# Group normalisation on one core: the store of the last tile but one in four parts on two queues

## The chip, the core and the metric

The kernel runs on one core of a Trainium2 chip. The metric is the device time of one execution in microseconds (us). The kernel before was run three times: 631.46, 631.93 and 632.73 us, so its median is 631.93 us. One further execution was recorded by the hardware profiler; it took 633.28 us, and all durations below come from it.

## The reference

The input `x` has 128 samples of 1024 channels of 32 x 16 values in bfloat16. The channels of a sample form 32 groups of 32 channels. Each group is normalised by its own mean and variance, and each channel is then scaled and shifted:

```python
xr = x.reshape(B, G, C // G, H, W)                   # G = 32
mu = xr.mean(axis=(2, 3, 4), keepdims=True)
var = ((xr - mu) ** 2).mean(axis=(2, 3, 4), keepdims=True)
xn = (xr - mu) / jnp.sqrt(var + 1e-5)
out = xn.reshape(B, C, H, W) * g[None, :, None, None] + b[None, :, None, None]
```

Input and output are 134 MB each, and every byte of them crosses between HBM and SBUF once.

## The kernel before, in words

**Tiles.** A tile is four samples: 4 x 32 groups lie on the 128 partitions, and each partition (a "row" below) holds the 32 x 512 = 16384 values of one group, 32,768 bytes, which lie together in HBM. A tile is 4 MB, and there are 32 (`NT`), numbered 0 to 31. Six buffers `x0` to `x5` (`SLOTS`) hold tiles in turn. A tile is normalised in place and stored from the buffer that it was loaded to.

**Work on one tile.** TensorE adds up the tile by 32 matmuls into one PSUM bank (`sums`). ScalarE makes a rough mean of one channel and then four passes of squares over the tile (`squares`, L228). VectorE joins the two to mean, variance, scale and shift (`normalise`, L244 to L284), and then writes 32 pieces of 128 x 512 in place (L294); the last of these raises `s_done` of the buffer.

**Queues.** All transfers of the kernel before are issued by SyncE (SP), in an order written out by hand (L147 to L155): the load of tile 0, two small loads of `g` and `b`, the loads of tiles 1 to 5; and then for every tile its store, followed by the load of the tile that comes five later. `load` (L132) waits until the store that last used the buffer has landed; `store` (L138) waits for `s_done` and issues one transfer of 128 rows (L141). After the last store, SP raises `s_gone` (L156) and waits until every buffer's stores have landed (L158); that wait ends the kernel. The two small loads read their source through `four`, which puts a dimension of four samples with step 0 in front, so that their outermost count is 4.

**GpSimd** makes the identity matrix at the start (L164 and L174), issues no transfer, waits for `s_gone` (L333) and clears semaphores.

A transfer raises its semaphore by 16 in all, whatever its size.

The functions that the change touches:

Of the kernel before, what the change touches and what calls it, by code (L numbers as in the profile page):

```python
# [11 lines left out]
BF16 = mybir.dt.bfloat16  # L12
# [4 lines left out]
SLOTS = 6  # L17
# [5 lines left out]
def kernel(  # L23
# [20 lines left out]
    NT = B0 // NS  # L44
# [4 lines left out]

    FIRST = -NT % SLOTS  # L50
    ROUNDS = (NT + FIRST) // SLOTS

    x_v = x.rearrange("(t n) (q k) h w -> t (n q) (k h w)", n=NS, q=G)
    o_v = out.rearrange("(t n) (q k) h w -> t (n q) (k h w)", n=NS, q=G)
# [7 lines left out]
    def sb(name, shape, dtype):  # L62
        return ctx.enter_context(nc.sbuf_tensor(name, shape, dtype))
# [7 lines left out]
    xs = [sb(f"x{j}", [P, F], BF16) for j in range(SLOTS)]  # L71
# [14 lines left out]
    ja = sb("ja", [P, HW], BF16)  # L86
    js = sb("js", [P, SQ], BF16)
    jd = sb("jd", [P, MM_FREE], BF16)
    jv = sb("jv", [P, SQ_PARTS], F32)

    def small(name, n=1):
# [13 lines left out]
    def sems(name):  # L105
        return [sem(f"{name}{j}") for j in range(SLOTS)]
# [13 lines left out]
    s_done = sems("done")  # L120
# [5 lines left out]
    s_eye = sem("eye")  # L126
    s_store = [tc.alloc_semaphore(f"store{j}") for j in range(SLOTS)]
    s_gone = tc.alloc_semaphore("gone")

    sp, pe, act, dve, pool = nc.sync, nc.tensor, nc.scalar, nc.vector, nc.gpsimd  # L130

# [6 lines left out]
    def store(i):  # L138
        j, n = (i + FIRST) % SLOTS, i // SLOTS
        sp.wait_ge(s_done[j], n + 1)  # L140
        sp.dma_start(out=o_v[i], in_=xs[j][:]).then_inc(s_store[j], 16)  # L141

    def four(v):
        return bass.AP(tensor=v.tensor, offset=v.offset, ap=[[0, NS]] + list(v.ap))
# [7 lines left out]
    for i in range(NT):  # L152
        store(i)
        if i >= 1 and i + SLOTS - 1 < NT:
            load(i + SLOTS - 1)  # L155
    sp.sem_inc(s_gone, 1)  # L156
    for j in range(SLOTS):
        sp.wait_ge(s_store[j], 16 * len(range((j - FIRST) % SLOTS, NT, SLOTS)))  # L158


    dve.memset(eps_t[:], EPS).then_inc(s_eps, 1)  # L161
# [3 lines left out]
        out=half[:],  # L165
        in_=ones[:],
# [8 lines left out]
        out=eye[:],  # L175
        in_=half[:],
# [128 lines left out]

    with pe.Fori(16, 16 * ROUNDS + 1, 16) as n16:
        m16 = pe.snap(n16 - 16)
# [5 lines left out]

    with act.Fori(1, ROUNDS + 1) as n:
        n16 = act.snap(n * 16)
        m, m16 = act.snap(n - 1), act.snap(n16 - 16)
# [5 lines left out]

    with dve.Fori(1, ROUNDS + 1) as n:
        m = dve.snap(n - 1)
# [5 lines left out]

    pool.wait_ge(s_gone, 1)  # L333
    pool.sem_clear(range(all_sems[0].num, all_sems[-1].num + 1))

# [29 lines left out]
```

## Time and profile before

| what | value |
|---|---|
| median of three runs | 631.93 us |
| the profiled execution, whole | 633.28 us |
| its span, as the profiler shows it | 631.6 us |
| bytes moved | 268.50 MB, 425 GB/s over the span |
| share of the 16 DMA engines' time that is busy | 98.9% |
| busiest compute engine | ACT, 519.4 us (82%) |
| VectorE | 394.9 us (63%) |
| TensorE | 287.4 us (46%) |
| GpSimd | 0.8 us |

How to read it: the span runs from the first to the last recorded instruction, and the whole time has 1.7 us more around it. The profile's chain of waits gives for the end of the execution what each step waited for. The view by stages gives for a stretch of the span the busy time of each engine and, in the last two columns, the share of the 16 DMA engines that was busy (1.00 is all of them; a packet is counted in the stretch in which it starts) and the GB/s that they moved. The trace also lists every DMA packet with its start, duration, size and queue, though not the DMA engine that moved it. Of the big transfers one packet is one row of 32,768 bytes; a transfer ends on each engine with one packet of 4 bytes, which counts up the semaphore.

### The profile page before, as it was taken

The page shows a single profiled execution, that of the slowest core. Times are in us where ns is not written, and L with a number is a line of the kernel's source. Part 1 is how long each engine was busy: PE and PEld are TensorE (multiplying, and loading weights), DVE is VectorE, ACT ScalarE, POOL GpSimd, SP SyncE. Part 2 cuts the span into 40 slices and gives each one's busy share as a digit, 9 for nine tenths or more (in the row PEclk, how much of TensorE's full clock was granted, in tenths as well). Part 3 has the DMA queues.
Part 4 walks back from the last instruction along what each step waited for, and adds up shares of the span by engine and source line. Part 5 has one row for each costly group of instructions (what it writes and reads, how often), then busy time and mean ns, then how long its engine had stood idle before and what let it go on. Part 6 is the DMA issues. An engine that isn't in the chain of part 4 may idle for free.

```text
span 631.6 us, 2995 instructions
## 1 busy us (share of the span) xinstructions
PE 287.4 (46%) x1024; PEld 3.3 (1%) x32; DVE 394.9 (63%) x1316; ACT 519.4 (82%) x354; POOL 0.8 (0%) x6
## 2 busy tenths in 40 slices
PE   1967605553255532455324654346553455533400
PEld 0000000000000000000000000000000000000000
DVE  0177777666666677777555775556765557755560
ACT  2999999999999999997879887889887898888800
POOL 0000000000000000000000000000000000000000
PEclk9999758756787667876678776777766787667755
DMA  8999999999999999999999999999999999999995
GB/s 363 432 430 417 436 436 432 430 430 434 428 432 432 432 432 432 430 432 430 430 434 434 436 432 432 438 434 436 430 431 434 434 432 432 434 432 432 432 432 235
DMA packets 9484, 268.50 MB, mean 425 GB/s; under 512 B 1288, under 2 KB 1288, under 8 KB 1288
## 3 DMA queue, kind: packets, MB, share of 16 engines
q1 hardware_dynamic: 9480, 268.46, 98.9%
q14 instruction: 3, 0.02, 0.0%
q8 instruction: 1, 0.02, 0.0%
HBM read 134.23 MB, written 134.22 MB: 425 GB/s over the span
## 4 chain that ended last, share of the span: by engine, by line
DMA 73%; ACT 18%; DVE 4%; issue 1%; SPq 1%; DVEq 0%; ACTq 0%
DMA out_dram<-x 67%; ACT js L228 17%; DMA x<-in_x_dram 7%; DVE x L294 3%; ACT ja L217 1%; SPq L136 1%; ACT std L237 0%; DVE jv L268 0%; DVE nd L259 0%; DVE d L255 0%; DVE bia L284 0%; DVE scl L280 0%; DVEq L58 0%; DVE rstd L278 0%; DVEq L254 0%
## 5 line engine op out<-in xcount | busy, mean ns | idle before, releaser
L228 ACT ACTIVATE js<-x,nshift 128x4096 bf16<-128x4096 bf16 x128 | 474.7, 3708 | 4.1
L294 DVE TENSOR_SCALAR x<-x,scl,bia 128x512 bf16<-128x512 bf16 x1024 | 333.7, 406 | 1.2
L193 PE MATMUL ps<-x,eye 128*128 128x512 bf16 x992 | 275.3, 447 | 0.0
L209 PE MATMUL ps<-x,eye 128*128 128x512 bf16 x32 | 18.6, 581 | 303.8 <-DMA x<-in_x_dram 303.8
L255 DVE TENSOR_TENSOR d<-negmean,nshift 128x1 f32<-128x1 f32 x32 | 5.1, 159 | 167.7 <-ACT js L228 167.7
L217 ACT ACTIVATE ja<-x 128x512 bf16<-128x512 bf16 x32 | 20.0, 624 | 48.7 <-DMA x<-in_x_dram 48.0
L244 DVE TENSOR_SCALAR_CACHE_REDUCE jd<-ps 128x512 bf16<-128x512 f32 x32 | 22.0, 686 | 16.4 <-PE ps L193 16.3
L237 ACT ACTIVATE std<-var,eps_t 128x1 f32<-128x1 f32 x32 | 9.4, 295 | 25.8 <-DVE jv L268 25.8
L228 ACT ACTIVATION_READ_ACCUMULATOR js<-x,nshift 128x1 f32 x128 | 23.9, 186 | 0.0
L278 DVE RECIPROCAL rstd<-std 128x1 f32<-128x1 f32 x32 | 5.2, 164 | 11.6 <-ACT std L237 11.6
L284 DVE SCALAR_TENSOR_TENSOR bia<-scl,negmean,bet 128x32 f32<-128x32 f32 x32 | 8.1, 252 | 1.1
L280 DVE TENSOR_SCALAR scl<-gam,rstd 128x32 f32<-128x32 f32 x32 | 7.7, 241 | 1.1
L186 DVE CAST gam<-gam_b 128x32 f32<-128x32 bf16 x1 | 0.2, 181 | 12.9 <-DMA bet_b<-in_b_dram 12.9
L268 DVE TENSOR_SCALAR_CACHE_REDUCE jv<-sq,nd 128x4 f32<-128x4 f32 x32 | 7.0, 217 | 1.1
L259 DVE TENSOR_SCALAR nd<-d 128x1 f32<-128x1 f32 x32 | 6.8, 214 | 1.1
L209 PEld LDWEIGHTS ps<-x,eye 128*128 128x128 bf16 x32 | 3.3, 103 | 578.7 <-DMA x<-in_x_dram 578.7
L217 ACT ACTIVATION_READ_ACCUMULATOR ja<-x 128x1 f32 x32 | 6.0, 187 | 0.0
L268 DVE DVE_READ_ACCUMULATOR jv<-sq,nd 128x1 f32 x32 | 2.7, 83 | 0.0
L244 DVE DVE_READ_ACCUMULATOR jd<-ps 128x1 f32 x32 | 2.6, 82 | 0.0
L184 ACT ACT_TABLE_LOAD x1 | 1.3, 1283 | 1.0 <-ACTq L58 1.0
L161 DVE MEMSET eps_t<- 128x1 f32 x1 | 0.1, 59 | 1.1 <-ACTq L58 1.1
L164 POOL TENSOR_SCALAR_AFFINE_SELECT half<-ones 128x128 bf16<-128x128 bf16 x1 | 0.3, 292 | 0.9 <-DVE ones L162 0.9
(8 smaller groups left out, 1.2 us busy)
## 6 DMA issues: line engine op xcount, KB each, us to landing
x<-in_x_dram SPq DMA_DIRECT2D x32, 4096.0 KB, 29.2
out_dram<-x SPq DMA_DIRECT2D x32, 4096.0 KB, 38.3
gam_b<-in_g_dram SPq DMA_DIRECT2D x1, 8.0 KB
bet_b<-in_b_dram SPq DMA_DIRECT2D x1, 8.0 KB
```

The source lines that it names most:

```text
L136: sp.dma_start(out=xs[j][:], in_=x_v[i]).then_inc(s_load[j], 16)
L193: return pe.add_instruction(mybir.InstMatmult(name=nc.get_next_instruction_name(), ins=[pe.lower_ap(rhs), first.ins[1]], outs=[first.outs[0]],
L209: m = pe.matmul(out=ps[j][:], lhsT=eye[:], rhs=xs[j][:, 0:MM_FREE], start=True, stop=False)
L217: act.activation(out=ja[:], in_=xs[j][:, 0:HW], func=ACT.Identity, scale=-1.0 / HW, accum_out=nshift[j][:],).then_inc(s_shift[j], 1)
L228: act.activation(out=js[:], in_=xs[j][:, k * SQ : (k + 1) * SQ], func=ACT.Square, bias=nshift[j][:], scale=1.0, accum_out=sq[j][:, k : k + 1],
L237: act.activation(out=std[j][:], in_=var[j][:], func=ACT.Sqrt, bias=eps_t[:], scale=1.0).then_inc(s_std[j], 1)
L244: dve.tensor_scalar(out=jd[:], in0=ps[j][:], scalar1=-inv_n, scalar2=None, op0=ALU.mult, op1=ALU.add, accum_out=negmean[j][:],).then_inc(s ...
L259: dve.tensor_scalar(out=nd2[j][:], in0=d[j][:], scalar1=d[j][:], scalar2=-1.0, op0=ALU.mult, op1=ALU.mult,).then_inc(s_nd2[j], 1)
L268: dve.tensor_scalar(out=jv[:], in0=sq[j][:], scalar1=inv_n, scalar2=nd2[j][:], op0=ALU.mult, op1=ALU.add, accum_out=var[j][:],).then_inc(s ...
L280: dve.tensor_scalar(out=scl[j][:], in0=gam[:], scalar1=rstd[j][:], scalar2=None, op0=ALU.mult).then_inc(s_scl[j], 1)
L284: dve.scalar_tensor_tensor(out=bia[j][:], in0=scl[j][:], scalar=negmean[j][:], in1=bet[:], op0=ALU.mult, op1=ALU.add,).then_inc(s_bia[j], 1)
L294: v = dve.tensor_scalar(out=xs[j][:, k * HW : (k + 1) * HW], in0=xs[j][:, k * HW : (k + 1) * HW], scalar1=scl[j][:, k : k + 1], scalar2=bi ...
```

## The change

Only the transfers around the store of tile 30 (`SHAPED = NT - 2`) are touched. SP issues rows 0 to 63 and rows 114 to 127 of that tile as two transfers in place of one. GpSimd issues rows 64 to 88 and rows 89 to 113, each as a transfer of 25 rows whose HBM side is written as 5 x 5 rows. Before the first of these GpSimd issues a load of 5 rows of 64 bytes into a new small tile `turn`, and between the two a load of one value of 2 bytes. GpSimd waits for `s_done` of tile 30 before its first 25 rows. SP's waits at the end also ask for the second part of that store and for the four transfers of GpSimd. The values computed are the same, and so is the order of all other transfers.

```diff
+    SHAPED = NT - 2
...
+    turn = sb("turn", [6, 32], BF16)
...
+    s_turn = tc.alloc_semaphore("turn")
+    s_fives = tc.alloc_semaphore("fives")
...
     def store(i):
         j, n = (i + FIRST) % SLOTS, i // SLOTS
         sp.wait_ge(s_done[j], n + 1)
-        sp.dma_start(out=o_v[i], in_=xs[j][:]).then_inc(s_store[j], 16)
+        if i != SHAPED:
+            sp.dma_start(out=o_v[i], in_=xs[j][:]).then_inc(s_store[j], 16)
+            return
+        rows(sp, i, 0, 64)
+        rows(sp, i, 114, 14)
+
+    def rows(engine, i, r, m):
+        j = (i + FIRST) % SLOTS
+        engine.dma_start(out=o_v[i][r : r + m], in_=xs[j][r : r + m]).then_inc(s_store[j], 16)
+
+    def fives(i, r):
+        j = (i + FIRST) % SLOTS
+        pool.dma_start(
+            out=o_v[i][r : r + 25].rearrange("(a b) f -> a b f", a=5), in_=xs[j][r : r + 25]
+        ).then_inc(s_fives, 16)
...
     for j in range(SLOTS):
-        sp.wait_ge(s_store[j], 16 * len(range((j - FIRST) % SLOTS, NT, SLOTS)))
+        uses = len(range((j - FIRST) % SLOTS, NT, SLOTS))
+        parts = 1 if j == (SHAPED + FIRST) % SLOTS else 0
+        sp.wait_ge(s_store[j], 16 * (uses + parts))
+    sp.wait_ge(s_turn, 32)
+    sp.wait_ge(s_fives, 32)
...
+    j = (SHAPED + FIRST) % SLOTS
+    pool.dma_start(out=turn[0:5, :], in_=x_v[0][0:5, 0:32]).then_inc(s_turn, 16)
+    pool.wait_ge(s_done[j], SHAPED // SLOTS + 1)
+    fives(SHAPED, 64)
+    pool.dma_start(out=turn[5:6, 0:1], in_=x_v[0][5:6, 0:1]).then_inc(s_turn, 16)
+    fives(SHAPED, 89)
+
     pool.wait_ge(s_gone, 1)
```

## The prediction

> **What bounds the kernel.** I read the share of the DMA engines first, then SP's waits at the end, then the end of the span by stages. The page's slices and queues:
>
> ```profile
> DMA  8999999999999999999999999999999999999995
> ...
> q1 hardware_dynamic: 9480, 268.46, 98.9%
> ...
> q8 instruction: 1, 0.02, 0.0%
> ...
> DMA 73%; ACT 18%; DVE 4%; issue 1%; SPq 1%; DVEq 0%; ACTq 0%
> ```
>
> The DMA engines are busy in every slice but the last, and 73% of the chain that ended last is DMA. ACT, the busiest compute engine at 82%, has slack. So only fewer or better placed bytes can help, and the one slice with room is the last. SP's waits from 600 us on, and the stages of the end (the last two columns are the DMA share and GB/s):
>
> ```profile
> SPq L158 <- DMA out_dram<-x: 19.5, 3, 9.6
> ...
> 590.90:610.30 19.40, 0.29 (x2) 0.00 (x0) 12.38 (x41) 7.28 (x5) 0.00 (x0) 0.56 1.01 434
> 610.30:623.00 12.70, 0.00 (x0) 0.00 (x0) 0.00 (x0) 0.00 (x0) 0.00 (x0) 0.50 0.98 423
> 623.00:624.20 1.20, 0.00 (x0) 0.00 (x0) 0.00 (x0) 0.00 (x0) 0.00 (x0) 0.50 0.32 137
> 624.20:626.60 2.40, 0.00 (x0) 0.00 (x0) 0.00 (x0) 0.00 (x0) 0.00 (x0) 0.50 0.25 109
> 626.60:629.00 2.40, 0.00 (x0) 0.00 (x0) 0.00 (x0) 0.00 (x0) 0.00 (x0) 0.50 0.13 55
> 629.00:631.60 2.60, 0.00 (x0) 0.00 (x0) 0.00 (x0) 0.00 (x0) 0.00 (x0) 0.50 0.00 0
> ```
>
> SP waits 19.5 us at L158 for stores; nothing else is at work after 610.3. Until 623.0 all 16 DMA engines are busy (0.98). Then 0.32 x 16 = 5 packets start in 1.2 us, then four (0.25), then two (0.13): a few engines end up to 6 us after the rest, and the kernel waits for the last of them.
>
> Which they are I worked out from the trace's list of packets. In it a row of 32,768 bytes takes 1.213 us, and the next packet of the same engine starts 4 ns before that end, so one row costs 1.21 us. Strung end to start, the packets form 16 chains; each has 512 rows, 8 for every transfer of 128 rows, and one 4-byte packet after each 8. The ends of the chains, in us of the span:
>
> ```
> 11 chains    623.16 to 623.74 (the median of all 16 is 623.54)
>  1 chain     624.76   loses 1.4 us at 469.6 us, beside the only packet of queue q8 (16,384 bytes, 0.93 us)
>  4 chains    627.07, 628.85, 628.86, 629.90
> ```
>
> The four late chains lose 0.1 to 0.6 us at a time, all along the execution, in rows that take longer than 1.213 us: 4.8 to 7.0 us in sum, against 1.3 to 2.1 us for the others. The 256 packets of 64 bytes (the loads of `g` and `b`, outermost count 4) lie on four chains, three of them late ones. The fourth late chain and the fourth 64-byte chain can have changed places in the stringing near 60 us, where all rows took 1.3 to 2.4 us and two chains can't be told apart. I take them as one: **the four engines that served the loads with outermost count 4 are the four that end late.** I call them the first four.
>
> **The change part by part.** All 128 rows of tile 30 still go out, so the bytes stay; their share per engine changes.
>
> *Rows per engine.* 128 rows went to 16 chains and a count of 4 to four chains, so I read a transfer as spread over as many engines as its outermost count allows, up to 16, beginning with the first. Then 64 rows give 4 to each of 16, and 14 rows give one to each of the first 14. A transfer of 5 x 5 rows gives five rows to each of five engines. No row shows GpSimd's queue, nor which five it takes; the diff's counts 5, 5, 1, 5 add up to 16, so if the turns go round, the first small load takes engines 0 to 4, the first 25 rows 5 to 9, the single value 10, the second 25 rows 11 to 15. Of tile 30:
>
> ```
> engines        rows before   rows after    change
> 0-4, 10             8        4+1   =  5    -3 rows = -3.63 us
> 5-9, 11-13          8        4+1+5 = 10    +2 rows = +2.42 us
> 14, 15              8        4+5   =  9    +1 row  = +1.21 us
> ```
>
> The sum is 6 x 5 + 8 x 10 + 2 x 9 = 128.
>
> - *The late four* lose three rows: the last ends at 629.90 - 3.63 = 626.27.
> - *Ordinary engines with ten rows* end at 623.74 + 2.42 = 626.16 at the latest.
> - *The engine of the q8 packet* isn't among the first four. Of the other 12, eight get ten rows: if it is one of these, it ends at 624.76 + 2.42 = **627.18**. With nine rows it ends at 625.97, with five earlier than the rest.
>
> I take the likelier, 627.18, as the new end: 629.90 - 627.18 = **2.72 us** less. If that engine isn't one of the eight, the late one sets the end and the gain is 3.63 us.
>
> *Do the rows come in time?* Tile 30 is ready at 590.9 (SP's issue at 590.92), while an ordinary engine ends tile 31 at 623.54 and so begins tile 30 at 623.54 - 16 x 1.21 = 604.2. GpSimd has 13 us to issue four transfers; SP's issues take 0.33 to 0.72 us each in the trace. GpSimd's own price isn't in the trace: its lower bound is nothing, and even 5 us for each 25 rows stays under the cover. Beyond that cover, up to the issue of tile 31 at 610.3, a heavy engine would still find its other rows to do. Cover gone altogether would cost at most the five rows moved there, 6.05 us.
>
> *Light engines 4 and 10* end tile 30 at about 604.2 + 5 x 1.21 = 610.2; tile 31 is issued at 610.27, and the first load's first packet started 1.0 us after its issue. They idle 1 us and still end near 621: nothing.
>
> *SP* issues one transfer more (0.33 us) at 591.3, before it waits until 610.25 for tile 31: hidden. Its two added waits at L158 follow the waits for the last stores; the three such waits in the trace took 17 to 28 ns each, so under 0.1 us. Behind them stands only the end of the program.
>
> *The two small loads.* Packets of 64 bytes took 11 ns; five of them and the 4-byte ones cost an engine under 0.2 us even at ten times that. The first is issued behind L174, which ends at 2.0 us, with nothing behind it on GpSimd until 590.9; the second lies in the cover above. GpSimd's wait for `s_done` holds up only its own transfers and the clearing of semaphores, which waits for `s_gone` at 610.6 anyway.
>
> *Reading 64 rows through 16 engines.* Before, each engine moved the same rows of SBUF every time; now engines 0 to 15 all read from the lower half of the partitions, and ten of them also from the upper. If they get in each other's way, rows grow longer. Bounds: nothing, as a row took 1.21 us in load and store alike; or twice, the longest rows in the trace (2.43 us near 60 us). I take nothing, since 97% of the rows took 1.225 us or less, and keep the other for a rival. The Trainium skill speaks against me here: "SBUF — State Buffer", section "Door 1: The DMA port swizzle", says that partitions 0 to 63 reach only 8 of 16 ports, with 196 GB/s measured for 64 partitions against 328 for 128 (1 MiB each). By that page the 64 rows would run at about half rate, which would add some 4 rows, 4.8 us, and turn the gain into a loss of 2 us; no row of this trace has 16 engines reading half the partitions.
>
> The same skill ("DMA: Bandwidth & Descriptors", "Why a DMA increments its semaphore by 16 and not by 1") states that GpSimd's transfers on fewer than 16 engines take consecutive ones from a cursor that goes round. It also reports that some of GpSimd's plain copies are put on 16 engines with the rows rounded up, which would leave the cursor where it was; no run here shows either yet.
>
> **The sum.** 633.28 - 2.72 = 630.56 for the profiled execution. The median of the plain runs stands 1.35 us lower (631.93); the same gain gives **629.2 us**, 0.43% less. If all of that 1.35 us were lateness that only the profiled execution has, the last engine would end at 628.55 in plain runs and the gain would be 1.37 us: 630.6.
>
> **The rivals.**
>
> 1. *Shared reading, slower.* Rows of the 64-row part take up to twice as long. For: the packets near 60 us show that a row can take 2.43 us when all engines are disturbed. Against: everywhere else 16 engines hold 1.21 us. Price: four rows of 1.21 us more bring the heavy engine with the q8 packet to 627.18 + 4.84 = 632.02, 2.1 us after the old end: 634.0. If all ten rows of a heavy engine doubled, 627.18 + 12.1 = 639.28: 641.3. It decides once the four rows take 0.68 us more each (2.72 / 4).
> 2. *The turns stand otherwise, slower.* If the first 25 rows fall on late engines, the last ends at 629.90 + 2.42 = 632.32: 634.3. For: nothing in the trace fixes where the turns start. Against: the counts add to 16, so they start alike in each execution.
> 3. *The parts aren't spread as read.* If GpSimd's rows are dealt over all engines, the late ones keep eight rows (no change, 631.9) or get nine (+1.21, 633.1).
> 4. *The lateness isn't there to win.* It grows by chance in single rows; in plain runs it can be smaller or lie on another engine: 630.7 to 631.9.
>
> **Chances.** A measurement of this kernel tells about 0.2% (1.3 us) from no change. The forecast as worked out 0.50 (0.02 of it within 0.2%); rival 1 0.24; rival 2 0.12; rival 3 0.09 (0.05 no change, 0.04 slower); rival 4 0.05. So faster 0.48, same 0.02 + 0.05 + 0.05 = 0.12, slower 0.24 + 0.12 + 0.04 = 0.40. The likeliest case has 628.0 to 630.7: from 3.63 us of gain and a little less lateness, to the 1.37 us above. The range takes in rival 2, rival 3 and rival 1 with its four rows: 628.0 to 636.0. It leaves out the dearer half of rival 1 (0.12) and about 0.04 elsewhere.
>
> **What would show it.** Right: in the profile after, the DMA share falls from full to nothing within some 3 us around 624 to 627, not 6; strung packets show five rows of tile 30 on the four late chains; rows after 591 us keep 1.21 us. Rival 1: rows of 1.5 to 2.4 us after 591 us, and fewer GB/s there than 434. Rival 2: chains with ten rows among the late four, and an end near 632. Rival 3: no chain with five rows. Rival 4: the late chains are within 3 us of the others. My forecast is wrong if rows of the shaped tile slow down by over 0.68 us each, or if an engine of the late four gets GpSimd's rows.

## The result and the profile after

The changed kernel takes 648.53 us (median of four runs, 647.1 to 650.95) against 632.33 us before: 1.0261 times as long, interval 1.0221 to 1.0301. It is 16.2 us slower where 2.7 us of gain were forecast, and beyond the range of 628.0 to 636.0.

The page of the changed kernel, its slices of DMA share and GB/s and its queues:

```profile
DMA  8999999999999999999999999999999999999993
GB/s 366 439 421 417 423 437 433 429 441 423 437 431 429 441 423 435 437 421 445 429 429 441 425 437 433 429 443 423 434 439 425 445 423 435 437 423 402 289 253 156
...
q1 hardware_dynamic: 9444, 266.82, 97.3%
q0 software_dynamic: 160, 1.64, 1.1%
```

Up to the last slice the DMA engines are as busy as before, but in the three slices ahead of it they move 402, 289 and 253 GB/s at a share of 9 tenths or more. Busy engines that move less: that is the reading to learn here. GpSimd's queue is q0; its 1.64 MB are the 50 rows. The same by stages (the last two columns are DMA share and GB/s):

```profile
590.90:604.00 13.10, 0.00 (x0) 0.00 (x0) 6.75 (x24) 5.97 (x5) 0.45 (x1) 0.63 1.08 360
604.00:617.00 13.00, 0.00 (x0) 0.00 (x0) 4.93 (x16) 0.00 (x0) 0.00 (x0) 0.50 0.94 270
617.00:629.00 12.00, 0.00 (x0) 0.00 (x0) 0.00 (x0) 0.00 (x0) 0.00 (x0) 0.50 1.01 246
629.00:635.00 6.00, 0.00 (x0) 0.00 (x0) 0.00 (x0) 0.00 (x0) 0.00 (x0) 0.50 0.86 300
635.00:641.00 6.00, 0.00 (x0) 0.00 (x0) 0.00 (x0) 0.00 (x0) 0.00 (x0) 0.50 0.47 202
641.00:646.00 5.00, 0.00 (x0) 0.00 (x0) 0.00 (x0) 0.00 (x0) 0.00 (x0) 0.50 0.14 59
```

And of the kernel before, the stage to compare with:

```profile
604.00:617.00 13.00, 0.00 (x0) 0.00 (x0) 6.24 (x20) 0.00 (x0) 0.00 (x0) 0.50 1.01 434
```

With the share near 1, 434 GB/s became 270 and 246. The list of packets says how: of the 440 rows that start after 591 us, 143 took longer than 1.3 us (before: one of 437), and the longest 5.29 us. Strung end to start, no chain has gaps of more than 1 us in sum; the rows themselves are long. Their excess over 1.213 us sums to 216.8 us, 13.5 us for each of 16 engines. The chains end 13.7 us later on average (638.5 against 624.8 us) and the last at 645.9.

GpSimd itself was in time (its instructions in the changed kernel; L158 is the transfer of 25 rows):

```profile
589.84 0.52 POOL L158 DMA_DIRECT2D out_dram<-x  x1 [587.21 <-DVE x L317]
590.35 0.50 POOL L361 DMA_DIRECT2D turn<-in_x_dram  x1
590.84 0.51 POOL L158 DMA_DIRECT2D out_dram<-x  x1
```

It issued within 1.5 us, and its first row started at 594.25 us, 4.4 us after the issue, still beside tile 29.

### The profile page after: what moved, and what is told of

Same layout as the page of the kernel before. It is cut to its first block, busy times and chain, and to the rows that moved or that the text cites. A ratio compares the mean times of both kernels' runs of the same rounds, so it can differ in the third digit from the quotient of the medians.

```text
span 648.1 us, 3001 instructions
## 1 busy us (share of the span) xinstructions
PE 286.9 (44%) x1024; PEld 3.3 (1%) x32; DVE 394.7 (61%) x1316; ACT 519.3 (80%) x354; POOL 2.9 (0%) x10
## 3 DMA queue, kind: packets, MB, share of 16 engines
q0 software_dynamic: 160, 1.64, 1.1%
## 4 chain that ended last, share of the span: by engine, by line
DMA 71%; ACT 17%; DVE 4%; issue 1%; SPq 1%; DVEq 0%; ACTq 0%
DMA out_dram<-x 65%; ACT js L251 16%; DMA x<-in_x_dram 6%; DVE x L317 3%; ACT ja L240 1%; SPq L140 1%; ACT std L260 0%; DVE jv L291 0%; DVE nd L282 0%; DVE d L278 0%; DVE bia L307 0%; DVE scl L303 0%; DVEq L59 0%; DVE rstd L301 0%; DVEq L277 0%
## 5 line engine op out<-in xcount | busy, mean ns | idle before, releaser
L158 POOL DMA_DIRECT2D out_dram<-x x2 | 1.0, 516 | 587.2 <-DVE x L317 587.2
```

## The experiments

All change only the store of tile 30 (two repeat a small load instead). Times are medians, compared with the kernel before on the same chip; the ratio stands with its 95% interval.

| run | what goes out for tile 30 | us | before | ratio |
|---|---|---|---|---|
| e1 | SP: rows 0-63, then 64-127 | 647.10 | 632.13 | 1.024 (1.0215 to 1.0265) |
| e2 | SP: two halves of the columns | 632.75 | 632.13 | 1.0007 (0.9995 to 1.0019) |
| e3 | SP: even rows, then odd rows | 632.27 | 632.13 | 1.0003 (0.9992 to 1.0014) |
| e4 | GpSimd: the whole tile | 632.38 | 632.13 | 1.0007 (0.9994 to 1.0019) |
| e5 | SP: eight times 16 rows | 648.97 | 631.90 | 1.0262 (1.0241 to 1.0283) |
| e6 | the change's counts, every second row | 638.35 | 631.90 | 1.0099 (1.0079 to 1.0118) |
| e7 | e6, small loads in another order | 638.11 | 631.90 | 1.0091 (1.0069 to 1.0114) |
| e8 | SP rows 0-63 beside GpSimd 64-127 | 646.13 | 631.90 | 1.025 (1.0196 to 1.0304) |
| e9 | SP even rows beside GpSimd odd rows | 632.08 | 632.01 | 0.9998 (0.9987 to 1.0009) |
| e10 | SP: an eighth of the columns as 4 x 32 rows | 632.46 | 632.01 | 1.0003 (0.9993 to 1.0012) |
| e11 | e6, GpSimd's rows in ten fives | 650.82 | 632.01 | 1.029 (1.027 to 1.0309) |
| e12 | 16 more loads of `g`, at one place | 640.65 | 632.67 | 1.0123 (1.0106 to 1.014) |
| e13 | 16 more loads of `g`, one per tile | 636.20 | 631.86 | 1.0066 (1.0053 to 1.008) |

**Which part stretches the rows?** My theory after the result was rival 1, shared reading; the rivals were GpSimd's queue and the mere cutting of a store. e1 takes GpSimd away and keeps the halves:

```diff
-        sp.dma_start(out=o_v[i], in_=xs[j][:]).then_inc(s_store[j], 16)
+        sp.dma_start(out=o_v[i][0:64], in_=xs[j][0:64]).then_inc(s_store[j], 16)
+        sp.dma_start(out=o_v[i][64:128], in_=xs[j][64:128]).then_inc(s_store[j], 16)
```

> Tile 30 is stored by SP alone, rows 0 to 63 and then rows 64 to 127; GpSimd issues nothing. Theory A (shared reading): 16 engines read half of the partitions at a time, each row of tile 30 takes up to twice 1.21 us, so 8 x 1.21 = 9.7 us at most: 632.3 + 9.7 = 642 us, with rows of about 2.4 us before the end. Rival B (GpSimd's queue is what costs): no GpSimd rows, so as before, 632 us and rows of 1.21 us.

Measured: 15.0 us slower, without any GpSimd row. The stages of e1:

```profile
604.00:617.00 13.00, 0.00 (x0) 0.00 (x0) 5.37 (x17) 0.00 (x0) 0.00 (x0) 0.50 1.02 282
617.00:629.00 12.00, 0.00 (x0) 0.00 (x0) 0.00 (x0) 0.00 (x0) 0.00 (x0) 0.50 0.88 254
```

The same picture as the change: share 1.02, 282 GB/s. The chains end 8.8 us later on average, near the 9.7 us of doubled rows, but the last 12.2 us later in the profiled executions: the load is uneven, and single rows took up to 5.07 us. The halves alone nearly account for the result. e2 cuts by columns instead:

```diff
+        sp.dma_start(out=o_v[i][:, 0 : F // 2], in_=xs[j][:, 0 : F // 2]).then_inc(s_store[j], 16)
+        sp.dma_start(out=o_v[i][:, F // 2 : F], in_=xs[j][:, F // 2 : F]).then_inc(s_store[j], 16)
```

> Tile 30 is stored by SP in two transfers of all 128 rows, the first and the second half of the columns: as many bytes per transfer as in the halves by rows, but each engine reads its usual rows. Theory A (shared reading): as before, 632 us, packets of 16,384 bytes at 0.6 us. Rival C (a store cut in two costs in itself, whichever way): slower by as much as the halves by rows.

Measured: as before within the interval. Two transfers of 2 MB cost nothing if each holds all rows; rival C falls. e3 takes 64 rows at a time, but every second one:

```diff
+        sp.dma_start(out=o_v[i][0:P:2], in_=xs[j][0:P:2]).then_inc(s_store[j], 16)
+        sp.dma_start(out=o_v[i][1:P:2], in_=xs[j][1:P:2]).then_inc(s_store[j], 16)
```

> Tile 30 is stored by SP in two transfers of 64 rows, the even rows and then the odd rows, so that each transfer spans all partitions. Theory A1 (an engine pays when it reads where another engine reads at that moment, whatever the span): rows of tile 30 still meet in pairs, up to 9.7 us more, 638 to 642 us. Rival A2 (only the half of the partitions counts: a transfer that spans all of them is as fast as before): 632 us.

Measured: as before; theory A1 was wrong here. The stage of e3 that answers to e1's:

```profile
604.00:617.00 13.00, 0.00 (x0) 0.00 (x0) 4.27 (x14) 0.00 (x0) 0.00 (x0) 0.50 0.98 423
```

The same count, size and queue as e1, 423 GB/s in place of 282, and one row above 1.3 us. So 64 rows are not slow; 64 neighbouring rows are. e4 gives the whole tile to GpSimd:

```diff
+    pool.wait_ge(s_done[j], (NT - 2) // SLOTS + 1)
+    pool.dma_start(out=o_v[NT - 2], in_=xs[j][:]).then_inc(s_pool, 16)
```

> Tile 30 is stored whole, all 128 rows in one transfer, by GpSimd's queue in place of SP's. Theory A (shared reading): every engine reads its usual rows, so as before, 632 us, rows of 1.21 us; GpSimd's later start (its rows came 4.4 us after its issue) lies under the rest of tile 29. Rival B (GpSimd's queue costs): slower by 6 us or more.

Measured: as before. GpSimd's queue costs nothing in itself here.

**How fine is the grain?** e5 issues eight times 16 neighbouring rows:

```diff
+        for r in range(0, 128, 16):
+            sp.dma_start(out=o_v[i][r : r + 16], in_=xs[j][r : r + 16]).then_inc(s_store[j], 16)
```

> Tile 30 is stored by SP in eight transfers of 16 rows, 0 to 15, 16 to 31 and so on, one row for each engine. Theory H (each half of the partitions, 0 to 63 and 64 to 127, can be read at the rate of eight engines): the rate is as for the halves by rows, 216 GB/s while 16 engines read one half, and successive transfers of one half behave alike: about 642 to 648 us. Rival P (each small group of partitions can be read at the rate of one engine only, and 16 rows lie on four such groups): rows of four times 1.21 us, 3 x 9.7 = 29 us more, 655 to 662 us.

Measured: 649.0 us, 17.1 us slower: a little above theory H, well below rival P. Rows took up to 8.58 us, more than in e1, so something finer than the two halves probably counts as well. That the price stays below rival P may be because the engines drift apart and do not all read the same rows at once; no run shows that alone. Neither price was right. e8 puts the halves on two queues at the same time:

```diff
+            sp.dma_start(out=o_v[i][0:64], in_=xs[j][0:64]).then_inc(s_store[j], 16)
...
+    pool.dma_start(out=o_v[NT - 2][64:128], in_=xs[j][64:128]).then_inc(s_pool, 16)
```

> Rows 0 to 63 of tile 30 by SP and rows 64 to 127 by GpSimd at the same time, each spread over 16 engines. Theory H: GpSimd's rows begin beside the rest of tile 29, where the upper half is also read by its own eight engines, and SP's follow; rows stretch, but both halves are read at a time for a part of it: slower than before by less than the 15 us of the halves by rows, 638 to 646 us. Rival (two queues read both halves at once and nothing stretches): 632 us.

Measured: 14.2 us slower, at the upper end of the expectation; a second queue rescues next to nothing. e9 is e8 with every second row:

```diff
+            sp.dma_start(out=o_v[i][0:P:2], in_=xs[j][0:P:2]).then_inc(s_store[j], 16)
...
+    pool.dma_start(out=o_v[NT - 2][1:P:2], in_=xs[j][1:P:2]).then_inc(s_pool, 16)
```

> Tile 30's even rows by SP and its odd rows by GpSimd at the same time, 64 rows and four per engine each. If neither GpSimd's queue nor two queues at once cost anything, and only rows read across do: as before, 632 us, rows of 1.21 us; the loss of the interleaved form with 14, 25 and 25 rows (6 us) is then due to these counts. Rival (two queues at once stretch rows): 636 us or more, as the interleaved form.

Measured: no difference, one row above 1.3 us. Two queues at once are harmless here.

**Without the halves, does the lightening work?** e6 keeps every count of the change and takes every second row (`rows` and `fives` step by 2; GpSimd begins at rows 29 and 79, SP's 14 rows at row 1):

```diff
-        rows(sp, i, 114, 14)
+        rows(sp, i, 1, 14)
...
-            out=o_v[i][r : r + 25].rearrange("(a b) f -> a b f", a=5), in_=xs[j][r : r + 25]
+            out=o_v[i][r : r + 49 : 2].rearrange("(a b) f -> a b f", a=5), in_=xs[j][r : r + 49 : 2]
```

> The changed kernel with the same counts (64 and 14 rows by SP, twice 25 by GpSimd, the same turns), but each part takes every second row: SP rows 0, 2 .. 126 and 1, 3 .. 27; GpSimd rows 29, 31 .. 77 and 79, 81 .. 127. So an engine mostly reads the half of the partitions that it reads in a whole store. Theory H (only the two halves count): hardly a stretched row; the late engines have five rows and the forecast's sum holds, 2.7 us less, 629.6 us. Rival P (small groups count): the GpSimd rows still meet other engines at their groups, rows of 2.4 us, 635 to 645 us. Rival L (the late engines aren't the first four, or the turns stand otherwise): a late engine has ten rows, 634.7 us.

Measured: 6.4 us slower than before, 9.8 us better than the change (each against its own runs of before), but no gain. The stage of e6 beside the others:

```profile
604.00:617.00 13.00, 0.00 (x0) 0.00 (x0) 5.01 (x16) 0.00 (x0) 0.00 (x0) 0.50 0.99 343
```

Two things are in it. Rows still stretch: 343 GB/s at full share lies between e1 and e3, 83 rows took more than 1.3 us, 5.0 us per engine in sum. And the strung packets show where GpSimd's rows went, in e6 and in the changed kernel alike:

```
GpSimd's 50 rows per chain:   12 chains with 4, one with 2, three with none
the two chains without a row of SP's 14-row part (engines 14, 15):  none
the four chains with the 64-byte packets of g and b:  4 each
```

That is two transfers of 25 rows, each dealt two rows to an engine, 12 x 2 + 1: engines 0 to 12 if the dealing begins with the first, and not five engines with five rows. The first four have 4 + 1 + 4 = 9 rows of tile 30 in place of 8, where the forecast had 5. The four engines of e6 that stand 3.8 to 5.3 us behind the others at 590 us are, by the strung packets, the four that end last (633.7 to 636.0); the chains that got fewer rows end at 622.5 to 623.6 us. So the 6.4 us are about one row more on the late engines (1.2 us) and 5.0 us of stretching. e7 asks the same through the order on GpSimd:

```diff
-    pool.dma_start(out=turn[0:5, :], in_=x_v[0][0:5, 0:32]).then_inc(s_turn, 16)
...
     fives(SHAPED, 29)
-    pool.dma_start(out=turn[5:6, 0:1], in_=x_v[0][5:6, 0:1]).then_inc(s_turn, 16)
+    pool.dma_start(out=turn[0:5, :], in_=x_v[0][0:5, 0:32]).then_inc(s_turn, 16)
     fives(SHAPED, 79)
+    pool.dma_start(out=turn[5:6, 0:1], in_=x_v[0][5:6, 0:1]).then_inc(s_turn, 16)
```

> The interleaved form with the order on GpSimd turned round: 25 rows, the load of 5 rows, 25 rows, the load of one value. If the turns go round from engine 0 in each execution, the first 25 rows now fall on engines 0 to 4, the late ones, which have ten rows of tile 30: the last ends 2.42 us later than before, 634.7 us. Rival (the turns aren't dealt so, or start anywhere): as the interleaved form.

Measured: 638.11 us, as e6 (638.35). The order of the small loads sets nothing here. e11 cuts GpSimd's rows into fives, with small loads that would bring them to engines 5 to 9 and 11 to 15:

```diff
+    for t in range(5):
+        fives(SHAPED, 29 + 10 * t)
+        small(11)
+    small(6)
+    for t in range(5):
+        if t > 0:
+            small(11)
+        fives(SHAPED, 79 + 10 * t)
```

> The interleaved form with GpSimd's 50 rows in ten transfers of five rows, and between them small loads of 11 and 6 rows of 64 bytes, so that the counts would bring the first five transfers to engines 5 to 9 and the last five to engines 11 to 15 if GpSimd dealt a transfer of n rows to the next n engines. Theory T (turns go round by rows): the late engines have five rows of tile 30, ten chains have five rows of GpSimd's each; 629.6 us by the forecast's sum, up to 5 us more for rows read across. Theory F (a transfer of five rows always goes to the first five engines): ten rows of GpSimd's on each of engines 0 to 4, which then have 15 rows of tile 30 in place of 8: 7 x 1.21 = 8.5 us more, 640 us or above.

Measured: 650.8 us, theory F, though 18.8 us slower where its seven rows make 8.5: 64 of the rows after 591 us also took longer than 1.3 us. The stages of its end:

```profile
610.00:630.00 20.00, 0.00 (x0) 0.00 (x0) 0.00 (x0) 0.00 (x0) 0.00 (x0) 0.50 0.69 251
630.00:638.00 8.00, 0.00 (x0) 0.00 (x0) 0.00 (x0) 0.00 (x0) 0.00 (x0) 0.50 0.32 131
638.00:644.00 6.00, 0.00 (x0) 0.00 (x0) 0.00 (x0) 0.00 (x0) 0.00 (x0) 0.50 0.25 104
```

A share of 0.32 is five engines of 16; from 630 us on five carry all that is left, GpSimd's rows among them until 646.6 us, nearly all at 1.21 us. Never are more than five of GpSimd's rows under way at once. Ten transfers went to the same five engines, whatever lay between.

**What do the counts mean, and which engines are late?** e10 writes the HBM side of a piece as 4 x 32 rows:

```diff
+        c = F - F // 8
+        sp.dma_start(out=o_v[i][:, 0:c], in_=xs[j][:, 0:c]).then_inc(s_store[j], 16)
+        sp.dma_start(
+            out=o_v[i][:, c:F].rearrange("(a b) f -> a b f", a=4), in_=xs[j][:, c:F]
+        ).then_inc(s_store[j], 16)
```

> SP alone: tile 30 goes out as all rows with seven eighths of the columns, and then the last eighth of the columns of all rows, with the HBM side written with an outermost count of 4, so that four engines carry it: they have 7 + 4 = 11 rows' worth in place of 8, the other twelve 7. If these four are the ones that end late, the last ends 3 x 1.21 = 3.6 us later: 635.5 us, or a little more where rows are read across. Rival (the late engines are others): the late ones are relieved of one row, 630.7 us.

Measured: no change, neither expectation. If four engines had carried the piece, the other twelve would have lost one row and ended 1.2 us earlier; but eleven chains end at 623.2 to 623.7 us as before, and the last at 628.2. The piece went over all engines, eight of its packets on each chain. My reading is that 4 x 32 rows that lie evenly count as one run of 128 rows, and a 5 x 5 view as one run of 25, while the four of `g` and `b` has step 0 and can't be joined; no run tests this reading apart. e10 thus says nothing on which engines are late. e12 adds the load of `g` 16 times after tile 29's store:

```diff
+        if i == NT - 3:
+            for k in range(16):
+                sp.dma_start(out=again_b[:, k * KC : (k + 1) * KC], in_=four(g_v)).then_inc(s_again, 16)
```

> The kernel before, with the small load of g repeated 16 times into a spare tile after the store of tile 29 (its values are not used). The load of g puts 32 packets of 64 bytes, 7 ns apart, and one of 4 bytes on each of four engines: 16 of them add 16 x 0.23 = 3.7 us to these four. If they are the four that end late, the end comes 3.7 us later: 635.7 us. Rival (the late engines are others): these four end at 623.7 + 3.7 = 627.4 us of the span, before the late ones, and the time stays 632 us.

Measured: 8.0 us slower, for another reason. SP's queue and two stages of e12:

```profile
571.65 43.83 SPq L158 DMA_DIRECT2D again_b<-in_g_dram  x13
```

```profile
590.90:610.30 19.40, 0.03 (x1) 0.00 (x0) 12.37 (x41) 7.01 (x5) 0.00 (x0) 0.55 0.73 309
610.30:623.00 12.70, 0.00 (x0) 0.00 (x0) 0.00 (x0) 0.00 (x0) 0.00 (x0) 0.50 0.48 174
```

SP needed 43.8 us for 13 of these issues, so tile 30's store came late (issued at 617.3 us, before at 590.9), the DMA share fell to 0.48, and then all chains ended together at 637.7 to 637.9 us. So the time of e12 doesn't tell which engines are late, but its list of packets does. Each engine ends tile 29's store with a 4-byte packet: twelve engines at 603.9 to 604.5 us, the four late ones at 606.16, 608.97, 609.66 and 610.29. The load of `g` stands next in the queue, and its first packets of 64 bytes start 6 to 7 ns after the start of four of these: at 604.11, 604.54, 609.66 and 610.30. **Of the four engines that serve `g`, two are late and two are not; of the four late ones, two don't serve `g`.**

e13 spreads the loads over tiles 8 to 23 (`if 8 <= i < 24`, one each):

> As the run with 16 more loads of g, but one of them after the store of each of tiles 8 to 23, so that no queue has to hold them all at once. The extra 0.23 us per load lies on the four engines that serve an outermost count of 4. If these are the four that end late: 16 x 0.23 = 3.7 us later, 635.9 us, all four late chains later by that. Rival (the late engines are others): as before, 632 us, and the four 64-byte chains end at 627.4 us of the span beside the late ones.

Measured: 4.3 us slower (expected 3.7). Its stages after 610 us:

```profile
610.30:623.00 12.70, 0.00 (x0) 0.00 (x0) 2.78 (x9) 0.00 (x0) 0.00 (x0) 0.50 1.02 439
623.00:629.00 6.00, 0.00 (x0) 0.00 (x0) 0.00 (x0) 0.00 (x0) 0.00 (x0) 0.50 0.29 126
629.00:632.00 3.00, 0.00 (x0) 0.00 (x0) 0.00 (x0) 0.00 (x0) 0.00 (x0) 0.50 0.08 33
...
624.20:626.60 2.40, 0.00 (x0) 0.00 (x0) 0.00 (x0) 0.00 (x0) 0.00 (x0) 0.50 0.35 150
```

The common part still ends near 623 us, and the tail of a few engines now reaches 632.7 us (629.9 before). But neither expectation holds. If the four of `g` were the late four, four chains would end late, at about 631 to 634 us; if they were four others, eight would. Six do: at 627.3, 627.6, 628.5, 628.7, 630.2 and 632.7 us, and the share from 624.2 to 626.6 us is 0.35, six engines of 16, where it was 0.25 before. That is e12's overlap of two. Ahead of the first extra load, at 217 us, the four that serve `g` stand 0.0, 0.7, 2.7 and 4.1 us behind the bulk, and two that don't 1.1 and 3.3 us. In both runs the engine furthest behind serves `g`.

## Why the prediction was wrong

- *What bounds the kernel.* Right: the DMA engines to the end, and there a few late ones. That the late four are the four of `g` and `b` was a guess from the strung packets, and it is wrong: e12 and e13 show two of the late four among them.
- *"Reading 64 rows through 16 engines ... I take nothing".* **This step failed, and it makes most of the result.** e1, with nothing but it, is 15.0 us slower; e3, with 64 rows that are spread over the partitions, is unchanged. I chose the end at nothing because 97% of the rows ran at 1.21 us; but all of those belong to transfers of all 128 rows, so they couldn't speak on this question. The other end, twice, was too low as well: rows reached 5.29 us, and rival 1's dearest price, 641.3, was passed by 7 us. The Trainium skill's "SBUF — State Buffer", section "Door 1: The DMA port swizzle", which I had weighed and set aside, speaks of just such a loss: its 196 against 328 GB/s is a factor 0.60. The runs agree in size: e1 shows 282 against 434 GB/s, 0.65.
- *"Rows per engine".* **Failed too.** I read the 5 x 5 view as a count of five. GpSimd's 25 rows went two apiece to twelve engines and one to a thirteenth. The first four got nine rows, not five, and so did, by the strung packets, the four that end last in e6: rival 3 as described, with its 1.21 us instead of the 3.63 us of gain. So even with the reading unhindered there would have been no gain. And had the 5 x 5 view been dealt as I read it, the two late engines outside the first four would have had nine or ten rows, unless they happened to be engines 4 and 10. So the step that took the first four for the late four failed as well. The skill's page "DMA: Bandwidth & Descriptors", "Why a DMA increments its semaphore by 16 and not by 1", reports just this exception, with rows rounded up; the trace agrees (25 / 16 rounded up is 2). The cursor that it states for GpSimd's small transfers did not show: ten transfers of five rows used the same five engines (e11), which is what the same rounding up, to one row each, would give.
- *"Do the rows come in time?"* Right: 0.5 us per issue, the first row 4.4 us after its issue, all under the cover of tile 29. *SP's issues and the small loads*: SP's two issues took 1.6 us together, more than 0.33 each, and stayed hidden; e7 moved the loads without effect. That SP's issues take 0.33 to 0.72 us left out one of the trace before, a load's, that took 6.3 us.
- *The sum of the two.* With 64 rows harmless, the rest of the store as one part costs nothing (e3, +0.1 us) and as 14, 25 and 25 rows 6.4 us (e6); with the lower half as one part, 15.0 (e1) and 16.2 us (the change). The two don't add up (15.0 and 6.4 make more than 16.2); that both are rows that wait at the same partitions would explain it, but isn't shown.
- *Chances.* Rival 1 had 0.24 and a range that stopped at 636. Its upper bound came from the longest row of a trace that has only transfers of 128 rows, which says nothing on how much 16 engines hinder each other on 64.

Open: how the partitions are grouped for reading. Two halves alone don't explain e5's longest rows (8.58 us) nor e6's stretched ones; small groups as rival P prices them would have made e5 dearer. Open too is the side on which the rows wait: neighbouring rows are neighbours in SBUF and in HBM alike, in every run, so no run tells a wait at the partitions read from one at the addresses written. And which engines the other two late ones are, and why those four are late, no run shows. No version was faster than the kernel before: every part of a transfer that was found on fewer than 16 engines lay, as far as the strung packets tell, on the first ones, two of which are late, and the engines that it spared most in e6 (13 to 15) are not among the late ones, since they end first.

## What to carry to other kernels

Where a store like this one is cut, cut it by columns or by every second row, so that each part spans all partitions: the halves by neighbouring rows cost 15 us on 4 MB, those other two cuts nothing. Read the DMA share and the GB/s together: share near 1 with falling GB/s was here engines that hinder each other, and a second queue didn't help. And before a step relies on which engine carries what, string the packets of one run of that very form: the view of 5 x 5 rows in one piece went out as 25 rows.

## What the runs showed of the hardware that I had not expected

A single row of 32,768 bytes can take 5.3 us (the change) or 8.6 us (e5) in place of 1.21 us while its engine counts as busy. Thirteen issues of a small broadcast load in a row held SP's queue for 43.8 us (e12), though one such load took SP 0.72 us at the start and one per tile cost little more than its packets (e13). And a stop of all engines levels them: after it all 16 chains of e12 ended within 0.2 us, where they otherwise end 6 us apart.
